# Full-partition loads, packed keys in 64x32 tiles, and one exponential phase in mid-slot

## The chip, the cores and the metric

The kernel runs on one core of one Trainium2 chip. The metric is the device time of one execution in microseconds (us); lower is better.

Names used below: PE is the matmul engine, PEld its weight loads, DVE the vector engine, ACT the activation engine, POOL the third elementwise engine. "Clock" is the mean granted clock of PE, 1.00 being full speed. In the tile names, `a1T` and `a2u` are the exponentials of the first and the second attention, `sm` and `lns` the sums of the second and their logarithms, `a2n` its normalised weights, `ppT` the packed keys, `gT` the product h * cos(h), `ot` the output. The "tail" is the last 64 of the 576 rows.

## The reference

For each of 8 batches and 8 heads, 32 packed queries `p` attend over 576 keys; the 576 queries `q` then attend over the 32 results. Then comes a feed-forward layer with `h * cos(h)` in the middle.

```python
# q, k, v: (8, 8, 576, 64)   p: (8, 8, 32, 64)   float32
p_packed = sm_attn(p, k, v)                # softmax over 576 keys
out = sm_attn(q, p_packed, p_packed)       # softmax over 32 packed keys
x = out.transpose(0, 2, 1, 3).reshape(4608, 512)
h = x @ w_in                               # 512 -> 2048
return (h * np.cos(h)) @ w_out             # 2048 -> 512
```

## The kernel before

The kernel is a software pipeline over batches, which are called s. Work of one batch lasts one "slot", in which the h steps of batch s (matmul, Sin on ACT, product on DVE), the output matmuls of batch s-1 (the filler) and the attention of batches s+1 and s+2 are interleaved by hand. There is a manual schedule: every engine runs its instructions in the order of the program.

The packed keys are folded into the first layer: `PPW` is packed keys times `w_in`, and h is `PPW` times the normalised weights `a2n`. Two heads lie in a padded 128-row operand, so each piece takes two full matmuls for each of two groups:

```python
def pp_lhs(b, g, i):                                   # zero padded to 128 columns
    return ppT[b % 2][:, 2 * g + i, 64 - 64 * i:192 - 64 * i]

def ppw_piece(b, n, g, eng):
    ps = att.tile([128, 512], FP32, name="ppw", tag="att")
    for i in range(2):
        nc.tensor.matmul(ps, pp_lhs(b, g, i), w_in_bf[:, 2 * g + i, n * 512:(n + 1) * 512],
                         start=(i == 0), stop=(i == 1))
    # ... scaled copy to PPW by DVE or ACT
```

The softmax of the second attention divides by a sum that it turns into exp(-ln(sum)), both on ACT:

```python
def sums_main(b, g):
    ps = att.tile([128, 512], FP32, name="sm", tag="att")
    nc.tensor.matmul(ps, ones_blk, a2u[b][:, g, 0:512], start=True, stop=True)
    nc.scalar.activation(out=lns[b][:, g, 0:512], in_=ps, func=AF.Ln)

def normalise(b):
    nc.scalar.activation(out=lns[b], in_=lns[b], func=AF.Exp, scale=-1.0)
    for g in range(2):
        nc.vector.tensor_tensor(out=a2n[b][:, g], in0=a2u[b][:, g], in1=lns[b][:, g], op=ALU.mult)
```

The exponential phase stands at the head of each slot, and the h steps of the same batch wait for it:

```python
for s in range(1, B):
    s2_main(s, 0); s2_main(s, 1); fill(2)      # Exp -> a2u
    s2_tail(s); fill(2)
    s1_piece(s + 1, 0); fill(2)                # Exp -> a1T of the next batch
    s1_piece(s + 1, 1); fill(2)
    sums_main(s, 0); fill(2)                   # Ln -> lns
    sums_main(s, 1); sums_tail(s); fill(2)
    s1_piece(s + 1, 2)                         # Exp
    normalise(s); fill(16)                     # Exp, then DVE
    # ... 16 h steps with pp, PPW, transposes and the rest of the filler between them
```

Loads of k, q and v fill partitions 0 to 63 with one transfer and 64 to 127 with another, five row chunks against four (cut).

The softmax here doesn't subtract the row's maximum and nothing guards it: scores larger than these inputs give would overflow.

## Time and profile before

| | before |
|---|---|
| median time | 359.21 us (3 runs, 359.21 to 362.79) |
| PE busy / ACT busy / DVE busy | 80% / 60% / 52% |
| table loads on ACT | 32 of 1.283 us |
| a full slot | 36.1 us (mean of five, from phase head to phase head) |
| exponential phase of ACT, from its first table load to the end of the load for Sin | 10.6 us (median of five) |
| first h step | 35.0 us |

A table load (ACT_TABLE_LOAD) is an ACT instruction that stands in the built programs where ACT changes from one set of functions to another. The tables of the profile are read so: "PE 288.7 (80%) x2048" is busy time, share of the span, and number of instructions. In a line of a group, the count is followed by busy time in us and mean ns of one, then by the idle time of the engine just before them and what ended most of it. The clock line gives the granted clock in 40 equal slices, in tenths of full speed; a 9 is 90% or more.

Lines of the page of the kernel before (span, busy time by engine, clock, and two groups of instructions):

```profile
span 359.7 us, 5266 instructions
...
PE 288.7 (80%) x2048; PEld 146.1 (41%) x2048; DVE 188.7 (52%) x327; ACT 214.3 (60%) x320; POOL 64.0 (18%) x55
...
PEclk9996655768789999999999999999999999999998
...
L238 ACT ACTIVATE cosT<-hT,pihalf 128x512 bf16<-128x512 f32 x128 | 87.9, 687 | 85.8 <-PE hT L232 77.7
...
L170 PE MATMUL ppw<-w_in_bf,ppT_118 128*128 128x512 bf16 x64 | 20.9, 425 | 9.9 <-DVE w_in_bf L339 8.2
```

The page says that the clock is low mainly between about 27 and 108 us, and that ACT waits for PE's h steps (77.7 us of idle time) rather than the other way round. Windows of the kernel before, two slots; the columns are the stretch, its length, then busy time of PE, PEld, DVE, ACT, POOL, the clock, the DMA share and GB/s:

```profile
168.00:202.00 34.00, 31.04 (x248) 16.19 (x247) 20.46 (x37) 25.66 (x40) 7.33 (x6) 1.00 0.70 136
201.98:239.66 37.68, 34.76 (x265) 17.90 (x264) 21.98 (x39) 26.57 (x40) 7.34 (x6) 1.00 0.63 130
```

In both PE is idle for only 3 us and the clock is full: PE bounds the slots in the main. Timeline of ACT in the exponential phase of the second of them (start, duration, engine, line, instruction):

```profile
201.98 1.28 ACT L186 ACT_TABLE_LOAD   x1
203.27 0.69 ACT L186 ACTIVATE a2u<-s_2031,rinv 128x512 bf16<-128x512 f32 x1
...
205.94 1.28 ACT L206 ACT_TABLE_LOAD   x1
207.23 1.08 ACT L206 ACTIVATE lns<-sm 128x512 f32<-128x512 f32 x2
...
208.51 1.28 ACT L141 ACT_TABLE_LOAD   x1
209.80 0.38 ACT L141 ACTIVATE a1T<-s_2091 128x256 bf16<-128x256 f32 x1
...
211.73 1.28 ACT L238 ACT_TABLE_LOAD   x1
```

There are four loads: for Exp, Ln, Exp again, and Sin.

### The profile page before, as it was taken

How to read it: one execution, taken by the hardware profiler on the slowest of the kernel's cores; microseconds unless marked ns; L12 is line 12 of the kernel's file. 1: busy time of each engine (PE TensorE's matmuls, PEld its weight loads, DVE VectorE, ACT ScalarE, POOL GpSimd, SP SyncE). 2: the span in 40 equal slices, each digit the busy share in tenths (PEclk: the TensorE clock that was granted, in tenths of full speed). 3: DMA queues.
4: the chain of work that ended last, by engine and by line, in shares of the span. 5: the costliest groups of instructions: out<-in, count | busy, mean ns of one | idle time of the engine just before them, and what ended most of it. 6: DMA issues, size and time to landing. Idle time of an engine off the chain costs nothing.

```text
span 359.7 us, 5266 instructions
## 1 busy us (share of the span) xinstructions
PE 288.7 (80%) x2048; PEld 146.1 (41%) x2048; DVE 188.7 (52%) x327; ACT 214.3 (60%) x320; POOL 64.0 (18%) x55
## 2 busy tenths in 40 slices
PE   0464666665979988999899989988998899978995
PEld 0340222333435444545454445444544454434442
DVE  4243565627057844766187537752884376436500
ACT  1327333443756687557957885578668855886410
POOL 4211032524231420142014202310050000000000
PEclk9996655768789999999999999999999999999998
DMA  7997169986919921993199329920971111211243
GB/s 146 205 286 283 20 120 211 322 257 125 200 34 198 207 80 29 197 203 115 31 193 203 90 50 222 211 58 2 188 165 29 23 39 40 47 31 29 44 89 74
DMA packets 36377, 45.83 MB, mean 127 GB/s; under 512 B 4096, under 2 KB 27648, under 8 KB 36352
## 3 DMA queue, kind: packets, MB, share of 16 engines
q1 hardware_dynamic: 36352, 45.49, 59.3%
q8 instruction: 16, 0.26, 0.3%
q14 instruction: 9, 0.07, 0.1%
HBM read 36.04 MB, written 9.44 MB: 126 GB/s over the span
## 4 chain that ended last, share of the span: by engine, by line
PE 47%; ACT 21%; DMA 14%; DVE 9%; issue 4%; POOL 3%; SPq 2%; POOLq 0%; DVEq 0%; ACTq 0%
PE ot L265 21%; PE hT L232 13%; DMA raw<-in_q_dram 8%; PE ppw L170 5%; DMA raw<-in_k_dram 4%; PE tps L110 4%; DVE a2n L218 3%; ACT L206 3%; ACT a2u L186 2%; ACT lns L216 2%; ACT lns L206 2%; ACT a1T L141 2%; DVE gT L239 2%; PE ht L235 2%; ACT L186 2%
## 5 line engine op out<-in xcount | busy, mean ns | idle before, releaser
L238 ACT ACTIVATE cosT<-hT,pihalf 128x512 bf16<-128x512 f32 x128 | 87.9, 687 | 85.8 <-PE hT L232 77.7
L265 PE MATMUL ot<-w_out_bf,gT 128*128 128x512 bf16 x512 | 135.4, 382 | 0.0
L239 DVE TENSOR_TENSOR gT<-hT,cosT 128x512 bf16<-128x512 f32 x128 | 87.6, 685 | 29.0 <-ACT cosT L238 28.6
L232 PE MATMUL hT<-a2n,PPW 128*128 128x512 bf16 x256 | 84.5, 409 | 14.4 <-DVE a2n L218 8.3
L265 PEld LDWEIGHTS <-gT 128*128 128x128 bf16 x512 | 44.9, 98 | 39.7 <-issue 1.6
L218 DVE TENSOR_TENSOR a2n<-a2u,lns 128x576 bf16<-128x576 bf16 x16 | 13.1, 860 | 70.0 <-ACT lns L216 70.0
L235 PEld LDWEIGHTS <-PPW 128*128 128x128 bf16 x256 | 26.0, 103 | 45.9 <-issue 15.1
L232 PEld LDWEIGHTS <-PPW 128*128 128x128 bf16 x256 | 25.2, 101 | 44.5 <-issue 10.3
L177 DVE TENSOR_SCALAR PPW<-ppw,rinv 128x512 bf16<-128x512 f32 x36 | 26.8, 749 | 14.6 <-PE ppw L170 14.3
L235 PE MATMUL ht<-a2n,PPW 128*128 128x64 bf16 x256 | 29.9, 200 | 4.9 <-DVE joint L245 4.9
L170 PE MATMUL ppw<-w_in_bf,ppT_118 128*128 128x512 bf16 x64 | 20.9, 425 | 9.9 <-DVE w_in_bf L339 8.2
L175 ACT ACTIVATE PPW<-ppw,rinv 128x512 bf16<-128x512 f32 x28 | 19.1, 683 | 8.8 <-PE ppw L170 8.8
L170 PE MATMUL ppw<-w_in_bf,ppT_119 128*128 128x512 bf16 x64 | 19.7, 410 | 0.8 <-DVE ppT_119 L158 0.8
L273 ACT COPY osb<-ot 128x512 f32<-128x512 f32 x18 | 10.5, 583 | 16.2 <-PE ot L265 16.0
L88 POOL CAST vbf_117<-raw 128x2048 bf16<-128x2048 f32 x4 | 8.1, 2018 | 64.5 <-DMA raw<-in_v_dram 64.5
L271 DVE COPY osb<-ot 128x512 f32<-128x512 f32 x18 | 12.3, 683 | 12.0 <-PE ot L265 12.0
L88 POOL CAST vbf_116<-raw 128x2048 bf16<-128x2048 f32 x4 | 7.6, 1892 | 58.8 <-DMA raw<-in_v_dram 36.9
L119 DVE COPY kT<-tps 128x640 bf16<-128x640 bf16 x26 | 12.7, 489 | 8.7 <-PE tps L110 8.2
L110 PE MATMUL tps<-ident,kbf_112 128*128 128x128 bf16 x80 | 8.3, 264 | 10.4 <-DVE kbf_112 L88 6.3
L265 PE MATMUL ot<-w_out_bf,joint 128*128 128x512 bf16 x64 | 16.4, 379 | 0.0
L139 PEld LDWEIGHTS <-kT 128*128 128x128 bf16 x160 | 7.9, 102 | 18.3 <-issue 13.9
L117 ACT COPY kT<-tps 128x640 bf16<-128x640 bf16 x6 | 4.2, 692 | 18.6 <-PE tps L110 18.6
(172 smaller groups left out, 324.0 us busy)
## 6 DMA issues: line engine op xcount, KB each, us to landing
out_dram<-osb SPq DMA_DIRECT2D x72, 128.0 KB, 2.4
raw<-in_v_dram SPq DMA_DIRECT2D x8, 640.0 KB, 6.2
raw<-in_q_dram SPq DMA_DIRECT2D x8, 640.0 KB, 10.5
raw<-in_k_dram SPq DMA_DIRECT2D x7, 640.0 KB, 14.2
raw<-in_v_dram SPq DMA_DIRECT2D x8, 512.0 KB, 8.1
raw<-in_q_dram SPq DMA_DIRECT2D x8, 512.0 KB, 12.5
raw<-in_moe_w_in_dram SPq DMA_DIRECT2D x4, 1024.0 KB, 10.1
raw<-in_moe_w_out_dram SPq DMA_DIRECT2D x4, 1024.0 KB, 7.6
```

The lines of the kernel that those rows point to most:

```text
L88: eng.tensor_copy(out=dv[:, 0:4], in_=tv[:, 0:4])
L110: nc.tensor.transpose(ps[:, c, :], src[:, c, hp * 128:(hp + 1) * 128], ident)
L170: nc.tensor.matmul(ps, pp_lhs(b, g, i), w_in_bf[:, 2 * g + i, n * 512:(n + 1) * 512], start=(i == 0), stop=(i == 1))
L175: nc.scalar.activation(out=dst, in_=ps, func=AF.Copy, scale=r)
L177: nc.vector.tensor_scalar(out=dst, in0=ps, scalar1=r, scalar2=None, op0=ALU.mult)
L206: nc.scalar.activation(out=lns[b][:, g, 0:512], in_=ps, func=AF.Ln)
L218: nc.vector.tensor_tensor(out=a2n[b][:, g], in0=a2u[b][:, g], in1=lns[b][:, g], op=ALU.mult)
L232: nc.tensor.matmul(ps, PPW[b][:, g, fc * 128:(fc + 1) * 128], a2n[b][:, g, 0:512], start=(g == 0), stop=(g == 1))
L235: nc.tensor.matmul(tails[b][:, fc % 8, :], PPW[b][:, g, fc * 128:(fc + 1) * 128], a2n[b][:, g, 512:576], start=(g == 0), stop=(g == 1))
L238: nc.scalar.activation(out=cs, in_=ps, func=AF.Sin, bias=pihalf)
L239: todo = [lambda: nc.vector.tensor_tensor(out=gT[b][:, fc, :], in0=ps, in1=cs, op=ALU.mult)]
L265: nc.tensor.matmul(ps, src[:, fc, c * 128:(c + 1) * 128], w_out_bf[:, fc, :], start=(fc == 0), stop=(fc == NFC - 1))
```

## The change

Its intent: (1) make the loads use all 128 partitions with one large transfer each (and two small ones for the tail), for the first batch in the order k, q, v, with four raw buffers in place of three; (2) drop the zero padding and compute a piece with eight 64x32 tiles of the array, even heads in one row half and odd heads in the other; (3) gather all exponentials and logarithms of a slot in one phase in mid-slot, one batch ahead, so that no h step waits for its own softmax, with a dummy Ln meant to bring in one table for both functions. The diff, cut to its core:

```diff
-        for i in range(2):
-            nc.tensor.matmul(ps, pp_lhs(b, g, i), w_in_bf[:, 2 * g + i, n * 512:(n + 1) * 512],
-                             start=(i == 0), stop=(i == 1))
+    def octet(b, dst, rhs):
+        for hp in range(4):
+            for o in range(2):
+                nc.tensor.matmul(dst[o][32 * hp:32 * hp + 32], ppT[b][64 * o:64 * o + 64, hp, :],
+                                 rhs(hp)[64 * o:64 * o + 64], start=True, stop=True,
+                                 tile_position=(64 * o, 32 * hp))
 ... (loads, casts, transposes and scores in the new layout: cut)
+    def exp_table():
+        nc.scalar.activation(out=dummy, in_=pihalf, func=AF.Ln)
+    def exp_phase(b2, b1, f):
+        exp_table()
+        s2_piece(b2, False)                      # Exp -> a2u
+        fill(f)
+        s2_piece(b2, True)                       # tail scores, Exp
+        if b1 is not None:
+            s1_piece(b1, 0)                      # Exp -> a1T
+            fill(f)
+        sums_main(b2, 0)                         # Ln
+        fill(f)
+        sums_main(b2, 1)                         # Ln
+        if b1 is not None:
+            s1_piece(b1, 1)                      # Exp
+        fill(f)
+        sums_tail(b2)                            # Ln
+        if b1 is not None:
+            s1_piece(b1, 2)                      # Exp
+        fill(f)
+        normalise(b2)                            # Exp, DVE
 ... (start-up in a new order: cut)
     for s in range(1, B):
+        mid = 25 if n1 else 0
+        h_steps(s, range(0, 8), first, (total - mid) // 2)
+        if n1:
+            exp_phase(s + 1, s + 2 if n2 else None, 5)
+        h_steps(s, range(8, 16), second, filler[1])
```

## The prediction

> **What bounds the kernel now.** The page gives PE 80% busy, ACT 60%, DVE 52%. By windows: up to 90 us (first batch, attention of the second) nothing is full: latency chains, casts and loads, PE clock 0.67 from 40 to 90 us. From 90 to 337 us the seven slots are bound by PE: 34.2 to 37.7 us each, clock 1.00, PE busy 31.0 us of 34. A 512-column matmul starts every 0.216 us (timeline). PE's idle of about 3 us per slot lies mainly in the exponential phase at the slot's head, where ACT needs about 9.3 us, four table loads of 1.283 us among them, before a2n lets hT start. The end is 17.9 us of output matmuls and 4.4 us of copy and store.
>
> **What changes.**
> 1. *Packing.* A PPW or s2 piece is four matmuls of 512 columns (0.86 us); it becomes eight 64x32 tiles. The Trainium skill ("TensorE: Matmul & The Clock Gate", Part 3) says distinct tiles run concurrently; "TensorEngine Tiling (Array Packing)", Key Properties, says a mode switch drains the array. I estimate 0.6 us: about 1.3 us of PE less per slot. If the tiles of a row half serialise it is 1.1 us and a loss. No trace of before shows it.
> 2. *128-partition loads, new order, four raw buffers.* k, q, v arrive sooner: first hT at 30 to 31 us instead of 35. Splitting PPW between DVE and ACT takes about 0.7 us off each of three w_in rounds. In the slots loads are off the critical path.
> 3. *Exponential phase in mid-slot, one batch ahead.* Meant to need one table load for Ln and Exp (by the dummy Ln) plus one for Sin. The built program does not do that: each Exp after a Ln, and each Ln after an Exp, still has its own load. It has 55 loads where before has 32: seven per full slot instead of four. At 1.283 us that is +29.5 us of ACT in all, +3.8 us per full slot.
>
> **On the critical path.** ACT's exponential phase, added from measured durations (7 loads 9.0, a2u 1.9, a1T 2.1, Ln 1.5, reciprocal 1.2), takes about 16 us. In it PE has 25 output matmuls (5.4 us), scores, sums, and then only two h steps before it needs the hT buffers, for which Sin must be back: about 10 us of work in 17.5. So PE idles about 7 us per slot (plus 1 us at the joint tile) instead of 3, and gets 1.3 to 1.5 back: a full slot costs +2.5 to 3 us, five slots about +14. The first slot has an extra early exponential phase (three loads). Gains: hT of batch 1 starts near 85 us instead of 105 (partly a gain: its 28 output matmuls are still to do), the last slot has no exponential phase and runs at PE's rate (about 22 us instead of 26), slot 6 gains 2 to 3. Net: the start gives about 6 us, the end about 6, the middle takes about 17.
>
> **Prediction: 364 us, 8 in 10 between 351 and 377.** Faster by over 2%: 0.14; within 2%: 0.49; slower by over 2%: 0.37.
>
> **What would show it.** 55 table loads, about 71 us; ACT total about 240. PE busy lower by about 10 us. An eight-tile piece occupying 0.6 us. In mid-slot ACT without a gap for 15 to 17 us and PE waiting for a2u, a1T and cosT/gT; full slots of 37 to 40 us. First hT near 31 us.
>
> **What would make it wrong.** Tiles that serialise (+10 us or more); idle stretches of 3 us that lower the PE clock; a start that gains 12 us rather than 6; or PE work hidden under ACT's phase better than I count.

## The result, and the profile after

The changed kernel took 384.18 us (median of 4 runs, 383.92 to 386.85), against 360.25 us of the kernel before in the same rounds (4 runs, 359.21 to 362.79). The ratio is 1.067 with a 95% interval of 1.059 to 1.075: slower by 6.7%. All outputs are right. A ratio here is the mean time of one kernel's fast runs over the mean of the other's of the same rounds, so it is not quite the ratio of the medians quoted.

| | before | after |
|---|---|---|
| table loads | 32 | 55 |
| ACT busy, us | 214.3 | 248.6 |
| PE busy, us | 288.7 | 282.8 |
| mean clock of the span | 0.926 | 0.904 |
| first h step, us | 35.0 | 30.2 |
| full slot, phase head to phase head, us | 36.1 | 40.6 |
| exponential phase, measured as above, us | 10.6 | 17.4 |

The lines of the page of the changed kernel:

```profile
span 382.1 us, 5650 instructions
...
PE 282.8 (74%) x2208; PEld 140.7 (37%) x2208; DVE 183.5 (48%) x308; ACT 248.6 (65%) x374; POOL 60.4 (16%) x58
...
PEclk9999966655899699899989899999988998999999
...
L209 PE MATMUL ppw<-w_in_bf,ppT 64*32 64x512 bf16 x256 | 17.8, 460 | 17.6 <-DVE w_in_bf L115 9.2
```

The clock line now has dips (a 6, several 8s) all along the slots, where that of before is level. Windows of the changed kernel, two slots:

```profile
151.19:191.32 40.13, 32.69 (x277) 16.41 (x276) 21.12 (x36) 30.99 (x47) 6.13 (x6) 0.96 0.39 112
191.32:233.02 41.70, 33.31 (x275) 16.23 (x273) 20.68 (x36) 30.66 (x46) 6.72 (x7) 0.92 0.43 118
```

PE idles 7.4 and 8.4 us a slot where it idled 3 (over five slots 7.7 against 3.3), and the clock is below full. Timeline of ACT in the phase of the second of these slots:

```profile
191.32 1.28 ACT L261 ACT_TABLE_LOAD   x1
192.62 0.20 ACT L261 ACTIVATE dummy<-pihalf 128x1 f32<-128x1 f32 x1
192.84 1.28 ACT L237 ACT_TABLE_LOAD   x1
194.13 0.69 ACT L237 ACTIVATE a2u<-s_1997,rinv 128x512 bf16<-128x512 f32 x1
...
196.56 1.28 ACT L245 ACT_TABLE_LOAD   x1
...
200.77 1.28 ACT L174 ACT_TABLE_LOAD   x1
...
202.74 1.28 ACT L251 ACT_TABLE_LOAD   x1
...
204.33 1.28 ACT L183 ACT_TABLE_LOAD   x1
...
207.40 1.28 ACT L281 ACT_TABLE_LOAD   x1
```

Seven loads where there were four. The dummy Ln gets a load of its own, and the Exp right behind it gets another: what this program loads for the Ln doesn't serve the Exp. After that every change between the two functions is a load.

The timeline of PE in the same phase; the bracket gives the wait just before an instruction and what ended it:

```profile
194.87 0.19 PE L209 MATMUL s_2015<-qTt,ppT 64*32 64x64 bf16 x1 [2.73 <-ACT a2u L237]
...
197.75 2.15 PE L303 MATMUL ot<-w_out_bf,gT 128*128 128x512 bf16 x5
...
200.19 1.24 PE L303 MATMUL ot<-w_out_bf,gT 128*128 128x512 bf16 x5
...
205.95 0.63 PE L192 MATMUL pp<-a1T,vbf_114 128*128 128x64 bf16 x16 [1.73 <-ACT a1T L183]
...
210.16 1.01 PE L275 MATMUL hT<-a2n,PPW 128*128 128x512 bf16 x2 [2.68 <-DVE gT L282]
```

Five equal output matmuls take 2.15 us at 197.75 and 1.24 us at 200.19. Windows of 2 us around them show why (the figure after POOL's is the clock):

```profile
195.00:197.00 2.00, 1.64 (x20) 0.87 (x14) 0.00 (x0) 1.91 (x6) 0.00 (x0) 0.79 0.57 160
197.00:199.00 2.00, 2.00 (x6) 0.65 (x5) 0.00 (x0) 1.44 (x2) 1.65 (x1) 0.50 0.02 9
...
211.00:213.00 2.00, 2.00 (x14) 0.67 (x13) 1.47 (x3) 1.37 (x2) 0.00 (x0) 0.50 0.35 131
```

After the wait of 2.73 us, and again after the one of 2.68 us, the clock falls to half for a few microseconds, and PE works at half speed just when others wait for it: ACT waits 1.57 us for PE's sum ahead of its Ln at 200.16 us (its timeline). The Trainium skill, "TensorE: Matmul & The Clock Gate", Part 1, describes this: half clock after an idle window of about 3.4 us, and about 3.4 us of work to get it back. The trace agrees in kind. In length it does not quite: waits of 2.7 us were enough here, while one of 2.47 us (at 169.94 us) was followed by a clock of 1.00. Nor does the length of one wait decide: in e6 below, one of 1.62 us was enough.

### The profile page after: what moved, and what is told of

Same layout as the page of the kernel before. It is cut to its first block, busy times and chain, and to the rows that moved or that the text cites. A ratio compares the mean times of both kernels' runs of the same rounds, so it can differ in the third digit from the quotient of the medians.

```text
span 382.1 us, 5650 instructions
## 1 busy us (share of the span) xinstructions
PE 282.8 (74%) x2208; PEld 140.7 (37%) x2208; DVE 183.5 (48%) x308; ACT 248.6 (65%) x374; POOL 60.4 (16%) x58
## 4 chain that ended last, share of the span: by engine, by line
PE 54%; ACT 28%; DVE 10%; issue 4%; DMA 2%; ACTq 0%; DVEq 0%
PE ot L303 26%; PE hT L275 14%; PE tps L141 5%; ACT cosT L281 4%; DVE gT L282 3%; ACT L261 3%; ACT a2u L237 3%; PE ppw L209 3%; ACT lns L255 2%; ACT L237 2%; DMA p_raw<-in_p_dram 2%; ACT L174 2%; DVE PPW L224 2%; PE ht L278 2%; ACT L281 2%
## 5 line engine op out<-in xcount | busy, mean ns | idle before, releaser
L303 PE MATMUL ot<-w_out_bf,gT 128*128 128x512 bf16 x512 | 142.1, 403 | 0.0
L275 PEld LDWEIGHTS <-PPW 128*128 128x128 bf16 x256 | 25.6, 103 | 54.2 <-issue 25.2
L278 PEld LDWEIGHTS <-PPW 128*128 128x128 bf16 x256 | 26.6, 106 | 44.2 <-issue 13.4
L209 PE MATMUL ppw<-w_in_bf,ppT 64*32 64x512 bf16 x256 | 17.8, 460 | 17.6 <-DVE w_in_bf L115 9.2
L222 ACT ACTIVATE PPW<-ppw,rinv 128x512 bf16<-128x512 f32 x31 | 21.3, 686 | 13.8 <-PE ppw L209 13.7
L224 DVE TENSOR_SCALAR PPW<-ppw,rinv 128x512 bf16<-128x512 f32 x33 | 24.5, 748 | 11.0 <-PE ppw L209 10.8
L209 PEld LDWEIGHTS <-ppT 64*32 64x32 bf16 x384 | 7.4, 91 | 50.0 <-issue 42.1
L119 ACT COPY osb<-ot 128x512 f32<-128x512 f32 x18 | 10.6, 586 | 17.4 <-PE ot L303 17.2
L98 POOL CAST kbf_110<-raw 128x2048 bf16<-128x2048 f32 x4 | 7.6, 1893 | 73.0 <-DMA raw<-in_k_dram 72.8
L121 DVE COPY qT<-tps 128x1024 bf16<-128x1024 bf16 x14 | 9.7, 689 | 7.4 <-PE tps L141 7.2
L121 DVE COPY kT<-tps 128x1024 bf16<-128x1024 bf16 x14 | 9.7, 691 | 7.0 <-PE tps L141 7.0
L245 ACT ACTIVATE lns<-sm 128x512 f32<-128x512 f32 x16 | 9.2, 597 | 5.0 <-PE sm L244 4.9
L98 POOL CAST kbf_109<-raw 128x2048 bf16<-128x2048 f32 x3 | 6.0, 2006 | 40.7 <-DMA raw<-in_k_dram 31.7
```

What stands on the lines that cost most here:

```text
L121: eng.tensor_copy(out=out, in_=in_)
L209: nc.tensor.matmul(dst[o][32 * hp:32 * hp + 32], ppT[b][64 * o:64 * o + 64, hp, :], rhs(hp)[64 * o:64 * o + 64], start=True, stop=True, ti ...
L222: nc.scalar.activation(out=dst, in_=ps[g], func=AF.Copy, scale=r)
L224: engs[g].tensor_scalar(out=dst, in0=ps[g], scalar1=r, scalar2=None, op0=ALU.mult)
L275: nc.tensor.matmul(ps, PPW[b][:, g, fc * 128:(fc + 1) * 128], a2n[b][:, g, 0:512], start=(g == 0), stop=(g == 1))
L278: nc.tensor.matmul(tails[b][:, fc % 8, :], PPW[b][:, g, fc * 128:(fc + 1) * 128], a2n[b][:, g, 512:576], start=(g == 0), stop=(g == 1))
```

## The experiments

The theory after the first reading (T1): the change loses because the built program has seven table loads per slot rather than the intended two, which makes ACT's phase the critical path; PE's waits in it then cost twice, once as waiting and once as lost clock. The rivals: (R1) the tiled matmuls are the loss, by draining or serialising; (R2) the place of the phase in mid-slot is the loss, whatever its loads; (R3) the clock is only a symptom, and the ACT phase alone sets the time.

All twelve runs, with the kernel before in the same rounds at 359.7 to 361.4 us:

| run | median us | ratio to before (95%) | loads | slot us |
|---|---|---|---|---|
| changed kernel | 384.18 | 1.067 (1.059 to 1.075) | 55 | 40.6 |
| e1_joint | 329.63 | 0.913 (0.905 to 0.921) | 19 | 33.2 |
| e2_before_joint | 341.48 | 0.947 (0.939 to 0.955) | 16 | 33.9 |
| e3_nodummy | 362.94 | 1.005 (0.997 to 1.013) | 44 | 38.8 |
| e4_unpacked | 388.85 | 1.079 (1.070 to 1.088) | 55 | 41.5 |
| e5_warm | 373.42 | 1.032 (1.025 to 1.039) | 55 | 38.9 |
| e6_fill8 | 379.42 | 1.052 (1.048 to 1.055) | 55 | 40.7 |
| e7_joint_unpacked | 333.69 | 0.924 (0.921 to 0.927) | 19 | 33.9 |
| e8_joint_fill7 | 329.59 | 0.913 (0.909 to 0.918) | 19 | 33.4 |
| e9_fill_waits | 360.34 | 0.996 (0.988 to 1.004) | 55 | 37.0 |
| e10_joint_best | 323.59 | 0.896 (0.889 to 0.903) | 19 | 32.6 |
| e11_before_joint_order | 342.98 | 0.949 (0.940 to 0.957) | 16 | 33.9 |
| e12_warm_start | 380.88 | 1.055 (1.047 to 1.062) | 55 | 41.2 |

"Slot" is the mean of the five full slots. Gains quoted in us below are differences of medians, often between rounds, in which the kernel before moved by 1.7 us. Those of e4, e6 and e12 against the changed kernel, and of e7 against e1, are below 2%, but in each of these pairs the four runs of one don't overlap those of the other.

### e1: the joint table set, named

```diff
     def exp_table():
-        nc.scalar.activation(out=dummy, in_=pihalf, func=AF.Ln)
+        nc.scalar.preload_act_table_set("natural_log_exp_and_others")
```

> The changed kernel, with the dummy Ln replaced by an explicit load of the table set that holds both Ln and Exp: 19 table loads instead of 55, two per full exponential phase instead of seven, everything else as it is. Theory A (the table loads lengthen ACT's phase, PE waits for it and loses clock): ACT's phase shrinks by about 6.6 us, PE's idle per slot falls from about 7.5 us to under 2.5 and its clock stays at 1.00; five full phases, the early one, the short last one and the start together give about 38 us: 346 us (338 to 354). Theory B (the packed tiles and their mode switches cost the time): only a small gain, 375 us or more. Theory C (a phase in the middle of the h steps costs in itself, because hT's buffers are held up): 365 to 375 us.

Measured: 329.63 us, 54.6 us less than the changed kernel and 8.7% less than the kernel before. The direction was right, the size far above what was expected. ACT is busy 49.3 us less (199.3 against 248.6), and the mean clock is 0.951 instead of 0.904. The timeline of ACT in one phase of this run:

```profile
165.53 1.28 ACT L261 ACT_TABLE_LOAD   x1
166.82 1.68 ACT L237 ACTIVATE a2u<-s,rinv 128x512 bf16<-128x512 f32 x4
168.57 0.66 ACT L174 ACTIVATE a1T<-s 128x256 bf16<-128x256 f32 x2
169.86 0.60 ACT L245 ACTIVATE lns<-sm 128x512 f32<-128x512 f32 x1 [0.64 <-PE sm L244]
...
174.46 1.28 ACT L281 ACT_TABLE_LOAD   x1
```

Exp and Ln alternate without a load: two loads per slot, a phase of 10.2 us. ACT now waits for PE inside the phase (0.64 us here), and the clock of the slots is 1.00. The window of this slot:

```profile
165.53:198.69 33.16, 30.06 (x275) 15.43 (x273) 20.58 (x36) 23.73 (x40) 6.72 (x6) 1.00 0.56 150
```

This refutes R2 as the cause of the loss: the same phase in the same place, without its extra loads, belongs to a kernel that beats the one before. (e7 below adds that its full slots are no longer than those of e2.)

### e2: the joint table set in the kernel before

```diff
+    nc.scalar.preload_act_table_set("natural_log_exp_and_others")   # at the start, and once more ahead of batch 1
     ...
     for s in range(1, B):
+        if s > 1:
+            nc.scalar.preload_act_table_set("natural_log_exp_and_others")
         s2_main(s, 0)
```

> The kernel before, with the same joint table set loaded at the head of each slot: 16 table loads instead of 32, two per slot instead of four. It says how much of e1 is worth having without the rest of the change. Theory A: each slot's exponential phase shrinks by 2.6 us and PE, idle 3 us per slot, gets about 2 of them back: 345 us (340 to 350). If e1 is then as fast or slower than this, packing, loads and mid-slot phase are worth nothing; I expect e1 faster by 0 to 2%.

Measured: 341.48 us, within the expected range. The kernel before gains 5.3% by the same edit (its slots go from 36.1 to 33.9 us), so most of what e1 gains over the kernel before isn't due to the change. With the set named in both, the change takes the time from 341.5 to 329.6 us: the change without its extra table loads is a gain of 11.9 us, 3.5% where 0 to 2% was expected.

### e3: without the dummy Ln

```diff
     def exp_table():
-        nc.scalar.activation(out=dummy, in_=pihalf, func=AF.Ln)
+        pass
```

> The changed kernel without the dummy Ln: 44 loads instead of 55, six per full phase instead of seven, 1.5 us less ACT work per phase, nothing else changed. A dose below e1. Theory A: 384 less 8 to 16 us, 372 us (368 to 377). Theories B and C: within 3 us of 384.

Measured: 362.94 us, 21.2 us less, more than expected. Eleven loads and ten dummies are gone, and ACT is busy 16.3 us less (232.3 against 248.6). So a microsecond of ACT taken out of the phase was worth 1.3 us of time. A chain that only got shorter would give back 1 at most; the mean clock goes up with it (0.904 to 0.914), which fits T1 but by itself doesn't prove it.

### e4: the tiles undone in the changed kernel

```diff
-        for hp in range(4):
-            for o in range(2):
-                nc.tensor.matmul(dst[o][32 * hp:32 * hp + 32], ...,
-                                 tile_position=(64 * o, 32 * hp))
+        for g in range(2):
+            for i in range(2):
+                nc.tensor.matmul(dst[g], ppT[b][:, 2 * g + i, 64 - 64 * i:192 - 64 * i],
+                                 rhs(2 * g + i), start=(i == 0), stop=(i == 1))
 ... (zero-padded layout of ppT and the column order of a1T as before the change: cut)
```

> The changed kernel with the eight 64x32 tiles of a PPW or s2 piece undone: four matmuls on the whole array with zero-padded keys, as before the change; 55 table loads stay. The trace of the changed kernel shows a packed piece taking 0.34 us of PE from its start to the next matmul, where four matmuls took 0.86. Theory A: PE does 0.5 us more per piece, some of it hidden in the waits: slower than the changed kernel by 6 to 14 us, about 394 us. Theory B: faster, 375 us or less.

Measured: 388.85 us, 4.7 us more than the changed kernel. R1 is refuted: the tiles are a gain, though about half of what was expected. In the timeline of PE of the changed kernel an eight-tile piece took 0.34 us from its start to the next matmul (170.52 to 170.86 us), against 0.86 us (four times 0.216 us) for the four padded matmuls:

```profile
169.94 0.59 PE L275 MATMUL hT<-a2n,PPW 128*128 128x512 bf16 x2 [2.47 <-DVE gT L282]
...
170.52 0.41 PE L209 MATMUL ppw<-w_in_bf,ppT 64*32 64x512 bf16 x8
170.86 0.82 PE L303 MATMUL ot<-w_out_bf,gT 128*128 128x512 bf16 x3
```

The Trainium skill, "TensorE: Matmul & The Clock Gate", Part 3, says that distinct tiles run at the same time, and "TensorEngine Tiling (Array Packing)", Key Properties, says that a change of tiling mode drains the array. The first is seen here (eight matmuls of about 0.39 us each, all done in 0.41 us); a drain isn't seen apart, and what it costs is within those 0.34 us.

### e5: redundant matmuls in PE's waits

```diff
+    def warm(n, pool, tag, name):             # results are never read
+        ps = pool.tile([128, 512], FP32, name=name, tag=tag)
+        for _ in range(n):
+            nc.tensor.matmul(ps, ones_blk, w_out_bf[:, 0, :], start=True, stop=True)
 ... 10 before the tail scores, 6 before pp_piece, 10 before the third h step after the phase
```

> The changed kernel with all its 55 table loads, and redundant matmuls (results never read) put into three waits of PE in each mid-slot phase: 10 before the tail scores, 6 before the packed keys, 10 before the third h step after the phase; 26 x 0.216 = 5.6 us in waits that measured 2.7, 1.7 and 2.7 us. They add work and take no load away. In the changed kernel's trace the granted clock is 0.50 for about 3.4 us after the first and after the last of these waits, and the slot from 191.3 to 233.0 us has a mean clock of 0.92, that is 3.3 us of its 33.3 us of PE time. Theory A2 (beside the idle time, the lowered clock after it is what lengthened the slots beyond my prediction): mean clock of the slots back to 0.98 or more, slot 1 to 3 us shorter, 384 less 6 to 16 us: 373 us. Rival (the waits alone explain the time, the clock is a bystander, or the added matmuls only delay): 384 us or more.

Measured: 373.42 us. The same program with 26 useless matmuls more per slot is 10.8 us faster. Windows of this run, two slots:

```profile
149.75:188.58 38.83, 36.83 (x303) 18.53 (x302) 21.16 (x36) 30.91 (x48) 6.57 (x6) 1.00 0.40 114
188.58:227.30 38.72, 35.94 (x301) 18.13 (x299) 20.61 (x36) 30.57 (x46) 6.78 (x6) 1.00 0.48 129
```

PE is busy 36 to 37 us instead of 33, ACT is busy as before, the clock is 1.00, and the slot is 1.8 us shorter (38.9 against 40.6 in the changed kernel, five slots each). ACT's phase falls from 17.4 to 16.0 us, for ACT no longer waits for the sums of a PE at half speed. R3 is refuted: lost clock is a cost of its own.

### e6: a larger filler at every place of the phase (a miss)

```diff
-        mid = 25 if n1 else 0
+        mid = 40 if n1 else 0
-            exp_phase(s + 1, s + 2 if n2 else None, 5)
+            exp_phase(s + 1, s + 2 if n2 else None, 8)
```

> The changed kernel with 8 instead of 5 output matmuls at each of the five places of the phase: 40 of a slot's 64 or 80 under ACT's phase instead of 25, the same work in all, 55 table loads. Theory A: ACT's phase stays 16 us, but 3.2 us more of PE's work lies under it and the waits no longer lower the clock as much: slots of 41 us become 35 to 38, total 360 us (350 to 370). If the loads cost time in some other way than through PE's waits (rival): 380 us or more.

Measured: 379.42 us; the expectation was wrong. Slots stayed at 40.7 us. The timeline of ACT in one phase of this run shows where part of the gain went:

```profile
197.90 0.60 ACT L245 ACTIVATE lns<-sm 128x512 f32<-128x512 f32 x1 [1.35 <-PE sm L244]
199.84 0.60 ACT L245 ACTIVATE lns<-sm 128x512 f32<-128x512 f32 x1 [1.34 <-PE sm L244]
```

The extra output matmuls stand in front of the sums that ACT needs. In this phase, of 19.1 us, ACT waits 2.69 us for the two sums (1.72 us in the phase of the changed kernel shown, of 17.4 us), and PE's wait at its end, for the product of an h step, is 3.38 us. But the median phase of five is 17.4 us here too. The clock shows the rest: it is 0.92 in four of the five slots, so it was not held up. Timeline of PE in the same phase, and a window of 2 us there:

```profile
193.28 0.22 PE L209 MATMUL s<-qTt,ppT 64*32 64x64 bf16 x7 [1.62 <-ACT a2u L237]
...
194.22 3.43 PE L303 MATMUL ot<-w_out_bf,gT 128*128 128x512 bf16 x8
```

```profile
195.00:197.00 2.00, 2.00 (x6) 0.73 (x5) 0.00 (x0) 1.54 (x2) 0.62 (x1) 0.50 0.50 152
```

The three matmuls more at the first place shorten the wait from 2.73 to 1.62 us, and the clock still falls to half, just where the filler stands in front of the sums. Filling was useful in front of an instruction of PE that waits (e5, e9), not in front of one that another engine waits for.

### e7 and e8: the tiles and the filler, with the joint set

e7 is e1 with the tiles undone as in e4; e8 is e1 with 7 filler matmuls at each place instead of 5.

> e1 (19 loads) with the packed tiles undone: what packing is worth once the tables are right and PE bounds the slot. 0.5 us per piece, four PPW pieces per slot and one s2 piece that is hidden in a wait: +2 us for each of six slots and some at the start: 342 us (337 to 347) against 329.6. Rival (mode switches make the tiles worthless): within 3 us of e1.

> e1 with 7 instead of 5 output matmuls at each place of the phase, a try at a better version. e1's slot from 165.5 to 198.7 us has 3.1 us without PE work, 1.6 of them at the head of the phase, the rest at the hT buffers and the joint tile; up to 1 us per slot may be had: 324 us (320 to 330).

Measured: 333.69 and 329.59 us. e7 was a miss; e8 lies just inside its range, but the gain of 5 us that it forecast didn't come. The tiles are worth 4.1 us (1.2%), not 12. PE is busy about 32.2 us a slot without them and 30.6 with them, but its idle time goes from 1.6 to 2.6 us: more than half of the saved PE time turned into waits. A uniformly larger filler gave nothing. The gap between e2 and e7 (7.8 us) is what the new loads, the fourth raw buffer and the place of the phase give together. It isn't in the full slots, which last 33.9 us in both, so with the joint set the place of the phase costs a slot nothing that the other parts don't give back; the first h step comes 4.6 us earlier in e7 (27.7 against 32.3 us). These runs don't separate the parts further.

### e9: useful matmuls in the waits, with all 55 loads

```diff
 ... output matmuls in place of those of e5:
+        fill(f + 10 if f else 0)                        # before the tail scores
+        second.append(lambda: (fill(6), pp_piece(s + 2)))
+            if i == hot: fill(10)                       # before the third h step
 ... (the counts of the remaining filler: cut)
```

> The changed kernel with all of its 55 table loads, and with useful output matmuls put into the waits in the places where the warm run (373 us) put redundant ones: up to 10 more before the tail scores, 6 before the keys of the batch after, 10 before the third h step that follows the phase. If the lost clock and the empty waits were what the change cost, both come back: a slot of 38.9 us loses up to 5.6 us of separate output matmuls (26 times about 0.215 us), until the ACT work of about 30.7 us a slot is the bound: about 348 us, 340 to 356. Rival: the matmuls stand in front of sums that ACT waits for, as in the run with 8 matmuls at every place, and the phase grows by what they take: 373 us or more.

Measured: 360.34 us, between the two expectations: 23.8 us less than the changed kernel, level with the kernel before (0.988 to 1.004), but not 348. The slot is 37.0 us with a clock of 1.00; PE is busy about 32 us and ACT 30.5 in it. One of them:

```profile
145.47:182.04 36.57, 31.70 (x276) 15.81 (x275) 21.01 (x37) 30.53 (x46) 6.29 (x6) 1.00 0.45 127
```

So neither is full, and some 5 us of PE's idle time remain in many waits of 0.2 to 1.3 us. Placing the filler in front of the waits is worth 24 us; making it larger at each of the five places (e6) was worth 5.

### e10: the best of both

```diff
 # e1, and: 4 more output matmuls before the tail scores, 3 before the third h step
-        fill(f)
+        fill(f + 4 if f else 0)
+            if i == hot: fill(3)
 ... (the counts of the remaining filler: cut)
```

> The changed kernel with the joint table set named (329.6 us) and 4 more output matmuls before the tail scores and 3 before the third h step after the phase. Its slots of 33.2 us hold 2.6 us of PE idle time; 7 matmuls of 0.215 us fill 1.5 of it: 322 to 327 us if they fall into idle time. Rival: what is filled there comes back as another wait, as in the run with 7 at every place (329.6): 328 to 331.

Measured: 323.59 us (322.39 to 325.6), within the expectation and 10.4% faster than the kernel before. This is the fastest version found.

### e11: the load order alone, in the kernel before

```diff
 # e2, and:
+    raws["q", 0] = load_raw(q, 0)
     raws["v", 0] = load_raw(v, 0)
-    raws["q", 0] = load_raw(q, 0)
```

> The kernel before with the joint set named (341.5 us), and its first batch loading k, q, v in this order and not k, v, q, as the changed kernel does; the loads keep their 64 partitions. If the order alone brought the earlier start, the first h step comes about 4 us earlier and the time is about 338 us; if the 128-partition loads did it, 341 us stays.

Measured: 342.98 us against 341.48 of e2 (in another set of rounds); the first h step came at 35.0 us against 32.3. The order k, q, v alone brings no earlier start. The first h step is at 26.7 us in e1, so that gain lies in the other parts of the new start: the full-partition loads, the casts split over two engines, the issue from two queues. These were not tested one by one.

### e12: redundant matmuls in the waits of the start only

```diff
 # changed kernel, and 37 matmuls whose results are never read, between 62 and 99 us:
+            warm(8)                    # after the main scores of batch 1
+    warm(7)                            # before pp_piece(1)
+        warm((4, 6, 3)[n - 1])         # before the later PPW pieces of batch 1
+            first.append(lambda: (warm(9), pp_piece(2)))
```

> The changed kernel with 37 redundant matmuls of 512 columns in the waits of the start alone (62 to 99 us: 7 before the packed keys of batch 1, 8 after its main scores, 13 among its later weight pieces, 9 before the packed keys of batch 2), the slots left as they are. If the lower clock between 62 and 111 us [...]is what delays the first mid-slot phase from the predicted 103.5 to 110.9 us, that phase starts 3 to 6 us earlier, near 106, and the time is 378 to 381 us with the slots unchanged at 40.6. Rival: the start is set by its table loads, casts and loads, and PE's speed there doesn't matter, or the redundant matmuls stand in the way: the phase starts at 111 or later and the time is 384 us or more.

Measured: 380.88 us, within the expected range. Windows of the same stretch, first of the changed kernel:

```profile
62.00:110.00 48.00, 30.39 (x309) 18.00 (x307) 25.15 (x40) 33.53 (x52) 23.06 (x18) 0.70 0.75 213
```

and then of this run:

```profile
62.00:110.00 48.00, 36.11 (x387) 19.36 (x385) 25.70 (x43) 39.95 (x63) 21.73 (x18) 0.99 0.81 227
```

The clock goes from 0.70 to 0.99, the h steps of batch 1 start at 85.5 us instead of 88.4, and the first mid-slot phase at 104.5 instead of 110.9. (The 103.5 us in the expectation is from the working behind the prediction; its text gives only "near 85 us" for the h steps.) Of the 6.4 us won here, the median shows only 3.3: in this run the slots were 0.5 us longer (41.15 against 40.6; the clock is 0.92 in four of the five, against three in the changed kernel), for a reason that isn't known.

## Why the prediction was wrong

Predicted were 364 us with a range to 377; measured were 384.2. Point by point:

- **What bounds the kernel before, right in the main.** PE's slots at full clock, 3.3 us idle. But 2.3 us a slot could be had from ACT's phase (e2).
- **The table loads, right.** 55 loads, seven per full slot. e1 shows them to be the main cost: naming the set takes 54.6 us off (18.2 in the kernel before, e2), and turns the change into a gain. ACT's phase, predicted as about 16 us from its instructions alone, lasted 17.4, for it had to wait for PE's sums, up to 1.57 us; with the clock held up (e5) it is 16.0.
- **PE's idle time per slot, right.** Predicted about 7 plus 1 us; measured 7.4 and 8.4 us in the two slots shown, 7.7 over five.
- **The tiles: direction right, size wrong.** A piece takes 0.34 us, not 0.6, but the whole is worth 4 to 5 us in time (e4, e7), because more than half of the PE time saved falls into waits (e7).
- **The first h step, right:** 30.2 us (predicted 30 to 31), though which of the load changes brought it wasn't tested (e11 excludes the order alone, in the kernel before). The last slot, from 337.4 to 360.6 us, took 23.2 us (predicted about 22).
- **The step that failed: "a full slot costs +2.5 to 3 us, five slots about +14".** The slots cost +4.5 us each. The idle time came as predicted; what failed is that PE "gets 1.3 to 1.5 back". PE is busy 32.9 us a slot (32.8 in the kernel before), though the same work takes 30.6 us at a clock of 1.00 (e1): the sum added busy time and waits as if PE always ran at full clock. It had named "idle stretches of 3 us that lower the PE clock" as a danger and given them no term. With the clock held up by redundant work (e5) a slot is 38.9 us, which is before's 36.1 plus 2.7: the predicted sum. The missing term is the lost clock: 1.8 us a slot, about 9 us in five slots.
- **The same omission in the start.** "hT of batch 1 starts near 85 us" came true only with the clock held up (85.5 in e12; 88.4 in the changed kernel), and the first mid-slot phase came 6.4 us late.

In run time the clock was worth 10.8 us in and behind the slots (e5, whose start is not changed: clock 0.72 from 62 to 110 us) and 3.3 us in the start (e12). No run has both. If they add up, they cover 14 of the 20 us between prediction and measurement; the other 6 are not assigned.

## What to carry to other kernels

Count the function tables in the built program, not in the intent: here naming a table set that holds both functions was worth 18.2 us in the kernel before (16 loads fewer) and 54.6 us in the changed one (36 fewer, and ten dummies), which is 0.86 and 1.11 us for each microsecond by which ACT's busy time fell (21.1 and 49.3). Where PE waits for the loads and then loses clock, a microsecond of loads can cost more than a microsecond. When a change adds waits to PE, give them a second term for the clock that they cost, and test it with redundant matmuls in the waits: if adding work makes the kernel faster and the clock rises, as in e5 and e12, clock was being lost. Then put useful work exactly in front of the instructions that wait, never in front of those that another engine waits for.

## What the Trainium skill lacked or had wrong

- "ScalarE: Activation LUTs", Table sets: the hidden batching unit, says that ln then exp takes one load, as one set has both. In this case's built programs each change between Ln and Exp had its own load, 55 in all, until the joint set was named by hand (19 loads, 384.2 to 329.6 us). The page's rule to use that set (its Rules for kernel authors) is right; it doesn't say that it has to be named, or that a dummy Ln in front doesn't bring it in (e3: the dummy cost 21.2 us).
- "ScalarE: Activation LUTs", What ACT_TABLE_LOAD costs, gives about 1.28 us for a load plus about 1.38 us for a drain. The load took 1.283 us here, and the next activation started about 0.01 us after it (192.84 plus 1.28, then 194.13 us). The instruction before it had ended 0.02 us earlier. No drain was seen on either side.
- "TensorE: Matmul & The Clock Gate", Part 1, and its rule on idle gaps over about 3 us: here waits of 2.73 and 2.68 us, and one of 1.62 us in e6, were followed by a clock of 0.50, and one of 2.47 us was not, so the length of one gap doesn't decide. What would help is a rule for a busy share within a window (these runs don't give it), and the cure: 26 redundant matmuls of 512 columns per slot saved 10.8 us (e5), 37 in the start lifted its clock from 0.70 to 0.99 (e12).
- "TensorEngine Tiling (Array Packing)", Key Properties, names the drain of a mode switch without a figure. An eight-tile 64x32 piece amid full matmuls took 0.34 us from its start to the next matmul, whatever its switches cost within that.
